# Top-k attention and a mixture of experts in one kernel: another order of all steps on every engine

## The chip, the cores and the metric

The kernel runs on one core of a Trainium2 chip. The metric is the device time of one launch in microseconds (us), from the start of the program to its end. The five engines of the core are named as in the profile: PE (TensorE, matrix products), DVE (VectorE), ACT (ScalarE), POOL (GpSimd) and SP (SyncE, which issues nearly all DMA transfers here). Each engine works off its own list of instructions in order; semaphores make it wait for the others.

## The reference

Attention of 2 batches, 8 heads, 576 rows and 64 columns per head, in which each row keeps only its 32 largest scores, is followed by a mixture of 4 experts on all 1152 rows:

```
scores = scale * np.matmul(q, k.transpose(0, 1, 3, 2))
kth = np.partition(scores, -top_k, axis=-1)[..., -top_k:-top_k + 1]      # top_k = 32
scores = np.where(scores >= kth, scores, -1000000000.0)
attn = np.exp(scores - np.max(scores, axis=-1, keepdims=True))
attn = attn / (np.sum(attn, axis=-1, keepdims=True) + 1e-09)
x = np.matmul(attn, v)                       # then heads side by side: x is 1152 x 512
p = domain_probs / (domain_probs.sum(-1, keepdims=True) + 1e-09)
for e in range(4):
    h = np.maximum(x @ w1[e], 0.0)           # w1[e]: 512 x 1024
    out += p[:, e:e + 1] * (h @ w2[e])       # w2[e]: 1024 x 512
```

All data is float32. The kernel splits each operand of a product into a high and a low half-precision part and adds three products (high by high, high by low, low by high).

## The kernel before

The 1152 rows are cut into ten row tiles (of 128 rows, and of 64 at the end of each batch). A tile of 128 rows has 8 units, one for each head; a 64-row tile has 4 units. There are 72 units, numbered 0 to 71 in the order of the tiles. A unit passes through these steps, each of them a small function that issues to one or two engines:

- `emit_qk` (PE, L643): scores of the unit into a PSUM bank. There are two such banks, so the scores of unit u need the bank that unit u-2 has left.
- `topk_op` (DVE, L656, L658 and L660): four rounds that find the 8 largest values (MAX8) with three that strike them out in between (MATCH_REPLACE).
- `emit_nb` (L693 on ACT, or L696 on DVE or POOL, by the table NB): the bias; `emit_exp` (ACT, L700): the exponential.
- `emit_mask` (L707 on DVE, or L710 and L714 on ACT and L717 on POOL): keeps the exponentials of the top 32. The table MASKS says for each unit which.
- `emit_a` (L725 on ACT, L727 and L729 on POOL): high and low part of the weights A.
- `emit_at` (SP, L735): transposes A with one DMA.
- `emit_av` (PE, L765): A times V into a PSUM bank for four heads. There is one such bank, which is free for the next four heads when `emit_x_half` (DVE, L785, L787, L789) has read it.

When a tile has all heads, its rows go through the experts: `m1` (PE, L882 to L884), the high part of h (ACT, L893), the low part (DVE L903, or ACT L900 and POOL L907, by the table H_LO), `m2` (PE, L929), and the evacuation with the expert's weight (by the table EVAC). The expert weights are loaded once: 16 loads of 1 MB (SP, L342). Each weight matrix has a power-of-two scale from its sum of squares, a chain over engines: Gram product of 32 matmuls (PE, L498), diagonal (DVE, L504), sum (PE, L507), then three small steps (DVE, L280, L282, L285). Then come the splits into high and low part (ACT L533, POOL L536). The queries of each tile are loaded and split likewise (L357, L373 to L402).

The order is written out by hand. Each step function is a generator; a step is entered in a heap with a place for each of its instructions, and all instructions are issued in the order of these places. The places are the numbers of the table ISSUE, one tuple per step and one number per instruction:

```
while events:
    place, i, n, f, args = heapq.heappop(events)
    ...
    heapq.heappush(events, (ISSUE[i][n] if ISSUE else place + (wait or 0), i, n, f, ()))
```

All five engines keep this order.

Of the kernel before, what the change touches and what calls it, by code (L numbers as in the profile page):

```python
# [43 lines left out]
H_LO = ('pddd', 'dppppppp', 'ppppdppp', 'dpppppdp', 'dpdpppdp', 'ppppdppd', 'pppppppp', 'pppppppp', 'pppdpppp', 'pppp')  # L44

MASKS = 'ddddddddddddddddrrdrrrrrrrrdrrrrrrrrrrrdrdrrrrdrrrrdrrdrrrrrrdrrrrrrrrrr'
NB = 'aaaadddddddaddadddddaadaadaapdddpppapppdpaaapapaaappppppapppppappaaaaaaa'
# [6 lines left out]
EVAC = ('ddpp', 'ddpp', 'dddp', 'ddpp', 'dppp', 'dpdd', 'dddd', 'dddd', 'dddd', 'dddd')  # L54
KV1 = dict(k='aaaaadaa', v='aaaaaaaa')
# [1197 lines left out]
```

## Time and profile before

| | |
|---|---|
| median of 3 runs | 539.23 us (539.05 to 540.62) |
| profiled execution | 540.16 us, of it 538.4 us span |
| busy share of the span | PE 94%, DVE 81%, ACT 68%, POOL 67% |
| chain of waits by engine | PE 78%, DVE 14%, DMA 2%, ACT 2%, SP 2% |
| mean granted TensorE clock | 0.977 of full speed |

The span runs from the first to the last instruction that the profiler recorded; the execution's own time is a little longer. A share of busy time is an average over stages that have different limits, so the profile is read by stretches of the span, and then by the lists of single instructions. In those lists the bracket at the end of a row is the idle time of the engine just before the instruction, and what ended it.

### The profile page before, as it was taken

The numbers are of one execution on the slowest core, as the hardware profiler recorded it, in microseconds if no ns is written. First come the engines' busy times: TensorE is split into PE (matmuls) and PEld (weight loads), VectorE is DVE, ScalarE is ACT, GpSimd is POOL, SyncE is SP. The second block draws the span as 40 slices with busy tenths as digits, with TensorE's granted clock in tenths as the row PEclk, the third lists the DMA queues.
The fourth block names the chain that finished last, engine by engine and source line by source line (L and its number), as shares of the span: only waits on it lengthen the run. The fifth ranks groups of instructions, "written<-read, shape, count | busy, mean of one in ns | idle before, by whom it ended". The sixth has DMA issues, their size and how long they took to land.

```text
span 538.4 us, 16332 instructions
## 1 busy us (share of the span) xinstructions
PE 505.1 (94%) x6738; PEld 384.6 (71%) x6738; DVE 433.7 (81%) x969; ACT 365.0 (68%) x602; POOL 361.4 (67%) x397
## 2 busy tenths in 40 slices
PE   7887758699999999999999999999999999999996
PEld 5666644586778677777777678677777778667766
DVE  3999997999999999999999989999999686610101
ACT  2999997998777777897768666764656635442121
POOL 0499997999877677978967866574665754253211
PEclk9997798799999999999999999999999999999999
DMA  8999998552474277574553642452423322214001
GB/s 218 311 255 331 265 280 170 104 90 47 99 144 75 65 111 128 94 139 93 122 113 88 110 70 66 83 89 45 76 52 62 71 45 47 43 24 65 12 2 32
DMA packets 142779, 58.37 MB, mean 108 GB/s; under 512 B 130096, under 2 KB 134448, under 8 KB 142704
## 3 DMA queue, kind: packets, MB, share of 16 engines
q1 hardware_dynamic: 139280, 54.50, 49.9%
q10 hardware_dynamic: 3424, 2.82, 1.7%
q8 instruction: 53, 0.87, 0.7%
q14 instruction: 22, 0.18, 0.1%
HBM read 25.45 MB, written 2.36 MB: 52 GB/s over the span
## 4 chain that ended last, share of the span: by engine, by line
PE 78%; DVE 14%; DMA 2%; ACT 2%; SPq 2%; issue 1%; POOL 0%; DVEq 0%
PE m L929 34%; PE m L882 11%; PE m L883 11%; PE m L884 11%; DVE m L656 6%; PE av L765 5%; PE ps L643 5%; DVE w L660 3%; DVE w L658 2%; DVE w L707 2%; DMA at<-a 2%; DMA pn<-in_moe_domain_probs_dram 1%; ACT w L533 1%; ACT w L527 1%; PE m L940 1%
## 5 line engine op out<-in xcount | busy, mean ns | idle before, releaser
L884 PE MATMUL m<-xt,w 128*128 128x128 f16 (+1 forms) x1280 | 199.8, 215 | 0.1
L929 PE MATMUL m<-w,h 128*128 128x512 f16 (+1 forms) x912 | 191.4, 383 | 0.0
L882 PE MATMUL m<-xt,w 128*128 128x128 f16 (+1 forms) x1120 | 178.9, 215 | 0.0
L883 PE MATMUL m<-xt,w 128*128 128x128 f16 (+1 forms) x1120 | 178.8, 215 | 0.0
L656 DVE MAX8 m<-w 128x8 f32<-128x576 f32 x216 | 161.6, 754 | 3.2
L929 PEld LDWEIGHTS <-h 128*128 128x128 f16 (+1 forms) x912 | 81.6, 101 | 88.4 <-issue 2.2
L884 PEld LDWEIGHTS <-w 128*128 128x128 f16 x1280 | 124.0, 99 | 0.2 <-POOL w L536 0.2
L882 PEld LDWEIGHTS <-w 128*128 128x128 f16 x1120 | 108.8, 99 | 2.6 <-issue 1.0
L907 POOL TENSOR_TENSOR h<-hf,h 128x512 f16<-128x512 f32 x59 | 68.4, 1160 | 62.6 <-ACT hf L900 62.2
L883 PEld LDWEIGHTS <-w 128*128 128x128 f16 x1120 | 108.5, 99 | 1.6
L660 DVE MATCH_REPLACE8 w<-m,w 128x576 f32<-128x576 f32 x144 | 106.9, 742 | 0.0
L727 POOL TENSOR_TENSOR a<-w,a 128x512 f16<-128x512 f32 x68 | 78.9, 1161 | 32.9 <-ACT a L725 17.9
L700 ACT ACTIVATE w<-ps,nb,es 128x576 f32<-128x576 f32 x68 | 56.3, 829 | 52.3 <-DVE m L656 46.1
L717 POOL TENSOR_TENSOR w<-w,d 128x576 f32<-128x576 f32 x48 | 61.4, 1282 | 27.6 <-ACT d L714 27.5
L893 ACT ACTIVATE h<-m 128x512 f16<-128x512 f32 x72 | 42.4, 593 | 53.5 <-PE m L884 35.9
L656 DVE MAX8 m<-ps 128x8 f32<-128x576 f32 x72 | 54.3, 755 | 15.2 <-PE ps L599 8.2
L725 ACT ACTIVATE a<-w 128x576 f16<-128x576 f32 x68 | 45.9, 679 | 13.2 <-POOL w L717 12.0
L658 DVE MATCH_REPLACE8 w<-m,ps 128x576 f32<-128x576 f32 x72 | 53.8, 747 | 0.0
L643 PE MATMUL ps<-kt,qa 128*128 128x288 f16 x128 | 34.9, 292 | 10.9 <-DVE w L707 10.0
L765 PEld LDWEIGHTS <-at 128*128 128x128 f16 (+1 forms) x1008 | 36.9, 101 | 9.1 <-DMA at<-a 3.5
L765 PE MATMUL av<-vt,at 128*128 128x65 f16 (+1 forms) x1008 | 39.4, 196 | 3.2 <-DMA at<-a 3.2
L900 ACT ACTIVATE hf<-m 128x512 f32<-128x512 f32 x59 | 34.9, 591 | 7.5 <-POOL h L907 6.0
(166 smaller groups left out, 759.1 us busy)
## 6 DMA issues: line engine op xcount, KB each, us to landing
w<-in_moe_w_dram SPq DMA_DIRECT2D x16, 1024.0 KB, 8.1
qraw<-in_q_dram SPq DMA_DIRECT2D x8, 256.0 KB, 3.4
qb<-qa SPq DMA_DIRECT2D x16, 128.0 KB, 2.6
out_dram<-o ACTq DMA_DIRECT2D x8, 256.0 KB, 2.2
at<-a SPq DMA_TRANSPOSE x68, 3.3
vraw<-in_v_dram SPq DMA_DIRECT2D x2, 512.0 KB, 7.4
nraw<-in_v_dram SPq DMA_DIRECT2D x4, 256.0 KB, 2.9
kraw<-in_k_dram SPq DMA_DIRECT2D x4, 256.0 KB, 2.9
```

What stands on the lines that cost most here:

```text
L643: PE.matmul(ps[:, 0:288], lhsT=src[:, x, :], rhs=kt[x].rearrange("p c n -> p (c n)")[:, ks], start=(j == 0), stop=(j == 1))
L656: DVE.max(m, s_t[u] if r == 0 else w_t[u])
L658: DVE.match_replace(rows2(w_t[u]), m, s_t[u], NEG)
L660: DVE.match_replace(w_t[u], m, w_t[u], NEG)
L717: POOL.tensor_tensor(w, w, g, op=OP.mult)
L727: POOL.tensor_tensor(a[:, 640:1152], w[:, 0:512], a[:, 0:512], op=OP.subtract)
L765: PE.matmul(o, lhsT=att[:, blk, ps], rhs=r, start=(i == 0), stop=(i == len(seq) - 1))
L882: PE.matmul(o, lhsT=HI[e, 0, c][:, fc], rhs=xs(0, c), start=(c == 0), stop=False)
L883: PE.matmul(o, lhsT=HI[e, 0, c][:, fc], rhs=xs(1, c), start=False, stop=False)
L884: PE.matmul(o, lhsT=LO[e, 0, c][:, fc], rhs=xs(0, c), start=False, stop=(c == 3))
L907: POOL.tensor_tensor(h[:, 1], hf, h[:, 0], op=OP.subtract)
L929: PE.matmul(y[z * 64:z * 64 + M, :], lhsT=h_t[es, qd][:, p // 2, h0:h0 + M], rhs=w, start=(fc == 0 and p == 0), stop=(fc == 7 and p == 2))
```

## The change

Only tables change: ISSUE as a whole, and five smaller tables that say which engine does a step. By count, DVE has three more low parts of h (16 for 13), three evacuations fewer (14 for 17) and one mask fewer (23 for 24); the number of biases on DVE falls from 20 to 19. Every computed value stays the same. The diff of the small tables, and the first rows of ISSUE:

```
-H_LO = ('pddd', 'dppppppp', 'ppppdppp', 'dpppppdp', 'dpdpppdp', 'ppppdppd', 'pppppppp', 'pppppppp', 'pppdpppp', 'pppp')
+H_LO = ('pddd', 'dppppppd', 'dpppddpp', 'dpdppdpp', 'ppdpppdp', 'ppppdppd', 'pppppdpp', 'pppppppp', 'pppppppp', 'pppp')
-MASKS = 'ddddddddddddddddrrdrrrrrrrrdrrrrrrrrrrrdrdrrrrdrrrrdrrdrrrrrrdrrrrrrrrrr'
+MASKS = 'ddddddddddddddddrrdrrrrrrrrrrrrrrdrrrrdrrddrrrrdrrrrrrrrrrrdrrrrrrrrrrrr'
-EVAC = ('ddpp', 'ddpp', 'dddp', 'ddpp', 'dppp', 'dpdd', 'dddd', 'dddd', 'dddd', 'dddd')
+EVAC = ('ddpp', 'dppp', 'dppp', 'ddpd', 'dppp', 'dpdp', 'dddd', 'dddd', 'dddd', 'dddd')
-KV1 = dict(k='aaaaadaa', v='aaaaaaaa')
+KV1 = dict(k='aaaaaaaa', v='aaaaaaaa')
 ISSUE = [
-    (0,), (9,), (10,), (48,), (54,), (1, 2), (3, 4), (20, 23), (36, 47), (25, 28), (12,), (13, 14), (19, 22, 32, 39),
...
+    (1,), (7,), (9,), (42,), (59,), (0, 2), (3, 4), (20, 24), (35, 46), (30, 34), (12,), (13, 15), (18, 22, 28, 60),
...
```

NB, the table of the engine of each bias, changes in the same manner. What the numbers do is seen in the order of the instructions.

On PE, in the ramp, before the change. A row is a source line, an instruction, what it writes and what it reads. `m1_1173` and `m1_1255` take the Gram products of two weight matrices, `w30_907` and `w21_128`; `av_1210` is the A·V bank of units 4 to 7, and `at_1039`, `at_1245` and `at_1251` are the transposed weights of units 5, 6 and 4; `ps0_1295` takes the scores of unit 11; `m2_1324` is an expert product of the first tile (24 matmuls).

```order
L498 MATMUL m1_1173<-w30_907 128x128
...
L765 MATMUL av_1210<-vt_139,at_1039 128x65
...
L498 MATMUL m1_1255<-w21_128 128x128
...
L643 MATMUL ps0_1295<-kt7_138,qa_398 128x288
...
L765 MATMUL av_1210<-vt_139,at_1245 128x65
...
L507 MATMUL m1_1255<-gd_1293,ones_112 128x1
...
L929 MATMUL m2_1324<-w10_125,h_1165 64x512
...
L765 MATMUL av_1210<-vt_139,at_1251 128x65
...
L507 MATMUL m1_1173<-gd_1362,ones_112 128x1
```

The same place after the change; `at_1154`, `at_1165` and `at_1199` are those of units 5, 6 and 4, `ps0_1194` and `ps0_1304` the scores of units 10 and 11, and `m2_1349` is the expert product.

```order
L765 MATMUL av_1173<-vt_139,at_1154 128x65
...
L643 MATMUL ps0_1194<-kt6_137,qa_445 128x288
...
L498 MATMUL m1_1211<-w21_128 128x128
...
L498 MATMUL m1_1247<-w30_1026 128x128
...
L507 MATMUL m1_1211<-gd_1281,ones_112 128x1
...
L765 MATMUL av_1173<-vt_139,at_1165 128x65
...
L643 MATMUL ps0_1304<-kt7_138,qa_445 128x288
...
L765 MATMUL av_1173<-vt_139,at_1199 128x65
...
L507 MATMUL m1_1247<-gd_1312,ones_112 128x1
...
L929 MATMUL m2_1349<-w10_125,h_1171 64x512
```

The expert product stood ahead of the second L507 and now stands behind it; the scores of unit 11 stood ahead of the A·V product of unit 6 and now stand behind it; the scores of unit 10, which before stood ahead of all these rows, have both Gram products behind them.

On SP, the DMA issues of the same stretch before the change, with no row left out. `w21`, `w30` and `w31` are loads of expert weights, `at` the transposed weights of units 5, 6 and 4, `qa` a transpose of queries. `kt6_137` and a load of queries stand some rows ahead of it.

```order
L342 DMA w21_128<-in_moe_w2_dram 128x4x512
L342 DMA w30_907<-in_moe_w1_dram 128x2x1024
L735 DMA_TRANSPOSE at_1039<-a_816 128x9x128
L342 DMA w30_907<-in_moe_w1_dram 128x2x1024
L342 DMA w21_128<-in_moe_w2_dram 128x4x512
L342 DMA w31_908<-in_moe_w2_dram 128x4x512
L735 DMA_TRANSPOSE at_1245<-a_1043 128x9x128
L394 DMA_TRANSPOSE qa_1248<-qhl_881 128x8x128
L735 DMA_TRANSPOSE at_1251<-a_814 128x9x128
```

And after the change, the same stretch:

```order
L342 DMA w21_128<-in_moe_w2_dram 128x4x512
L735 DMA_TRANSPOSE at_1154<-a_826 128x9x128
L342 DMA w30_1026<-in_moe_w1_dram 128x2x1024 x2
L735 DMA_TRANSPOSE at_1165<-a_1011 128x9x128
L357 DMA qraw_1168<-in_q_dram 128x8x64
L394 DMA_TRANSPOSE qa_1188<-qhl_847 128x8x128
L735 DMA_TRANSPOSE at_1199<-a_822 128x9x128
L342 DMA w31_1027<-in_moe_w2_dram 128x4x512
```

The first load of `w31` stood ahead of the transpose of unit 6 and now stands behind that of unit 4; the load of queries also moves behind the transpose of unit 6.

On PE, far behind the ramp, before the change. `ps0_6204` takes the scores of unit 53, `av_6257` is the A·V bank of units 48 to 51, `at_6140` is of unit 48 and `at_6434` of unit 49:

```order
L643 MATMUL ps0_6204<-kt1_132,qa_5510 128x288
...
L929 MATMUL m2_6212<-w10_125,h_5870 128x512
...
L765 MATMUL av_6257<-vt_139,at_6140 128x65
...
L643 MATMUL ps0_6332<-kt2_133,qa_5510 128x288
...
L765 MATMUL av_6257<-vt_139,at_6434 128x65
```

And after the change; `av_6170` is the A·V bank of units 48 to 51, `at_6089` is of unit 49 and `at_6202` of unit 48, `ps0_6190` takes the scores of unit 53:

```order
L765 MATMUL av_6170<-vt_139,at_6089 128x65
...
L643 MATMUL ps0_6190<-kt1_132,qa_5505 128x288
...
L882 MATMUL m1_6210<-xt_5765,w11_126 128x128
...
L643 MATMUL ps0_6291<-kt2_133,qa_5505 128x288
...
L765 MATMUL av_6170<-vt_139,at_6202 128x65
```

Unit 49 was the last of its four to go through A·V and is now the first, and stands just ahead of the scores of unit 53.

## Rows read from the trace of the kernel before

**Rows 1.** Stretches: from:to, length, busy us (instructions) PE, PEld, DVE, ACT, POOL; PEclk, DMA, GB/s.

```profile
60.00:80.00 20.00, 13.63 (x288) 12.50 (x286) 19.76 (x49) 19.78 (x23) 19.67 (x14) 0.92 1.15 281
80.00:90.00 10.00, 10.00 (x111) 5.95 (x108) 6.45 (x22) 6.95 (x9) 9.82 (x10) 0.83 0.99 205
90.00:120.00 30.00, 21.30 (x418) 19.12 (x416) 29.79 (x71) 28.79 (x34) 27.03 (x20) 0.89 0.56 102
120.00:200.00 80.00, 80.00 (x988) 58.70 (x986) 78.27 (x177) 61.21 (x109) 62.76 (x67) 1.00 0.49 88
...
300.00:400.00 100.00, 100.00 (x1257) 75.43 (x1256) 93.54 (x191) 62.73 (x109) 65.45 (x81) 1.00 0.41 74
```

**Rows 2.** Pieces of the chain of waits: start, length (both us), what.

```profile
71.40 8.36 DMA at<-a
...
117.84 0.73 DVE w L707
...
118.61 0.65 PE ps L643 x4
```

**Rows 3.** DVE's list: start, length, line, operation, out<-in, shapes; idle before.

```profile
78.26 0.75 DVE L656 MAX8 m<-ps 128x8 f32<-128x576 f32 x1
...
85.72 0.16 DVE L280 TENSOR_SCALAR wpt<-m 128x1 int32<-128x1 int32 x1 [3.55 <-PE m L507]
```

**Rows 4.** PE's list from 79 to 90 us.

```profile
79.81 0.76 PE L765 MATMUL av<-vt,at 128*128 128x65 f16 x14 [3.21 <-DMA at<-a]
...
80.87 4.07 PE L929 MATMUL m<-w,h 128*64 128x512 f16 x24
...
85.33 0.36 PE L507 MATMUL m<-gd,ones 128*128 128x1 f32 x2
...
86.56 2.78 PE L929 MATMUL m<-w,h 128*64 128x512 f16 x24
```

**Rows 5.** Two weight loads: SP's list, then the transfers' KB and us to landing.

```profile
63.69 0.72 SPq L342 DMA_DIRECT2D w<-in_moe_w_dram  x1
64.46 1.62 SPq L342 DMA_DIRECT2D w<-in_moe_w_dram  x1
...
w<-in_moe_w_dram SPq DMA_DIRECT2D x1, 1024.0 KB, 10.2
...
w<-in_moe_w_dram SPq DMA_DIRECT2D x1, 1024.0 KB, 12.0
```

**Rows 6.** POOL: a weight split from its list; its longest wait, 80 to 128 us.

```profile
62.17 2.14 POOL L536 TENSOR_TENSOR w<-w 128x1024 f16<-128x1024 f32 x1 [0.23 <-ACT w L533]
...
POOL a L727 <- ACT a L725: 2.7, 1, 2.7
```

**Rows 7.** ACT's waits, 82 to 100 us: us in total, times, longest.

```profile
ACT w L527 <- PE ps L643: 1.5, 1, 1.5
ACT w L700 <- DVE wpt L280: 1.2, 1, 1.2
ACT w L700 <- DVE m L656: 1.1, 1, 1.1
ACT a L725 <- DMA at<-a: 0.4, 1, 0.4
```

**Rows 8.** The squares of v of the second batch: ns min/median/max, first and last start.

```profile
L461 ACT ACTIVATE nraw<-nraw x4: 720/728/757, 132.5 to 200.4; 128x640 bf16<-128x640 f32 x4
```

**Rows 9.** Lists of POOL, PE, DVE and SP, 329 to 346 us; the transpose's landing.

```profile
329.32 1.16 POOL L907 TENSOR_TENSOR h<-hf,h 128x512 f16<-128x512 f32 x1 [0.88 <-ACT hf L900]
...
335.34 0.29 PE L643 MATMUL ps<-kt,qa 128*128 128x288 f16 x1
...
339.51 0.41 DVE L789 TENSOR_TENSOR x<-av,r 128x256 f32<-128x256 f32 x1
...
345.25 2.32 SPq L735 DMA_TRANSPOSE at<-a  x1
...
at<-a SPq DMA_TRANSPOSE x1, 3.8
```

More of the change, by code (lines that the diff above doesn't have):

```diff
@@ L43 @@
 MANUAL = ('PE', 'DVE', 'Activation', 'Pool', 'SP')
-H_LO = ('pddd', 'dppppppp', 'ppppdppp', 'dpppppdp', 'dpdpppdp', 'ppppdppd', 'pppppppp', 'pppppppp', 'pppdpppp', 'pppp')
-MASKS = 'ddddddddddddddddrrdrrrrrrrrdrrrrrrrrrrrdrdrrrrdrrrrdrrdrrrrrrdrrrrrrrrrr'
-NB = 'aaaadddddddaddadddddaadaadaapdddpppapppdpaaapapaaappppppapppppappaaaaaaa'
+H_LO = ('pddd', 'dppppppd', 'dpppddpp', 'dpdppdpp', 'ppdpppdp', 'ppppdppd', 'pppppdpp', 'pppppppp', 'pppppppp', 'pppp')
+MASKS = 'ddddddddddddddddrrdrrrrrrrrrrrrrrdrrrrdrrddrrrrdrrrrrrrrrrrdrrrrrrrrrrrr'
+NB = 'aaaaddddddaddaadaddddpdpdadppadpapppaaapppppadaappdaaaaaaapapaaaaaapapaa'
 X_LO = 'pppppppppp'
```

316 rows, old and new, of the table ISSUE are left out of this document.

## Prediction

> **What bounds the kernel now.** I first read the busy time of each engine by stretches [rows 1]. From 60 to 80 us DVE is busy for 19.76 of 20 us while PE has 13.63; from 90 to 120 us DVE has 29.79 of 30 and PE 21.30. From 120 us on PE is full (80.00 of 80). So there are two stages: a ramp, in which DVE's top-k sets the pace, and a long stage in which TensorE never waits. The second begins where the chain of waits passes from DVE to PE [rows 2]: the mask of unit 15 starts on DVE at 117.84, the scores of unit 17 (L643, into the bank that this mask had read) start on PE at 118.61, and from there the chain is PE's until the end. The change leaves PE's work in the second stage as it is. So the time falls by as much as that mask ends earlier, provided that PE is fed as well as before.
>
> In the ramp there is one hole: from 80 to 90 us DVE is busy for 6.45 of 10 us [rows 1]. DVE's own list of instructions shows why [rows 3]: its L280, the first step of a weight scale, waits 3.55 us for PE's L507. PE's list tells what is ahead of that L507 [rows 4]: the A·V product of unit 6 (L765), which waited 3.21 us for its transposed weights and started at 79.81, then 24 matmuls L929 of the expert layer, 4.07 us of them, then A·V of unit 4, and only then, at 85.33, the L507. The same 24 matmuls take 2.78 us a little later; the granted clock from 80 to 90 us is 0.83 of full speed [rows 1], so part of the 4.07 is the clock after the idle time. The transpose of unit 6 was issued on SP at 71.40 and landed 8.36 us later [rows 2]. Ahead of it SP had issued 1 MB weight loads, the last two at 63.69 and 64.46, which landed 10.2 and 12.0 us later, at 73.9 and 76.5 [rows 5]. So the hole has two causes, a transpose behind weight loads and an L507 behind 24 matmuls.
>
> **What the change does there.** On PE the 24 matmuls move behind the second L507, and both Gram products L498 move behind the scores of unit 10. On POOL the two subtractions that finish unit 6 move ahead of three weight splits (2.1 us each, [rows 6]) and a q split. On SP the transpose of unit 6 then follows two loads of w30 and nothing else that is new: one 1 MB load and a q load fewer are ahead of it.
>
> When does that transpose land? Nothing in the trace shows it with this queue, so I bound it. At the earliest it takes 3.8 us as one on a freer queue does [rows 9]. It can be issued when POOL has finished unit 6: three splits and one more such step earlier than 71.4, some 7.5 us, so at about 63.9, and lands at 67.7. At the latest it lands as before, at 79.76. The loads landed 2.6 us apart; with one fewer ahead the last of them lands at 73.9, and the transpose at most 3.3 us later, as before (79.76 − 76.5): 77.2. DVE wants the scores of unit 11, now behind that A·V product, at about 77.6: before, this MAX8 started at 78.26 [rows 3], and one MATCH_REPLACE of 0.74 us that was ahead of it is now behind. With 0.76 us for A·V [rows 4] and 0.65 for the scores [rows 2] the transpose must be there by 76.2. At 77.2 it costs 1.0 us, at 76.2 or earlier nothing. The L507 is wanted four top-k instructions of 0.7 us after 77.6, at about 80.4. With the 24 matmuls no longer ahead it needs only A·V of unit 4, whose transpose follows some 2 us behind (2.32 us is what SP takes to issue one, [rows 9]): at the latest 77.2 + 2.0 + 0.76 + 0.36 = 80.3, so it fits too.
>
> The Trainium skill, in "DMA: Bandwidth & Descriptors", section "Queues, rings and completion order", says that completion is not in order of issue for one issuing engine. By that the transpose need not wait for the loads ahead of it at all; here the landings of 73.9, 76.5 and 79.76 came in the order of issue [rows 2, 5]. By the rule the transpose would land near 67.7 and the first rival below would lose its chance; the sum below would stay, since it is capped elsewhere.
>
> **The sum.** On DVE the hole of 3.55 us goes, and ahead of the mask of unit 15 stand two reciprocals and two biases fewer and one L280 more, about 0.1 us each (an L280 is 0.16 us, [rows 3], and overlaps its neighbour): 3.55 + 0.3 = 3.9, less at most 1.0 for the late transpose, gives 2.9 to 3.9. But DVE is not alone. ACT works almost without a gap in the ramp; between 82 and 100 us it waited 1.5, 1.2, 1.1 and 0.4 us [rows 7], 4.2 in all, and can give back no more than these. The change puts one squaring of v (0.72 us and about 0.2 for its sum, [rows 8]) and small things of 0.2 ahead of the exponential of unit 15: 3.1 are left. POOL waited 2.7 us once, for ACT [rows 6], and has the same 73 instructions ahead of the last weight split, which PE needs early in the second stage: 2.7 and a little more. I take 2.8.
>
> Later, in the stage where PE is full, one step is tight. The A·V product of unit 49 moves eleven steps forward on PE, to just ahead of the scores of unit 53, which started at 335.34 [rows 9]. It is now the first to write the one A·V bank, and so must wait for DVE's L789 to have read the half before, which ended at 339.92 [rows 9]. The change moves that L789 ahead of three MAX8 and two MATCH_REPLACE, 5 × 0.75 = 3.75 us, so it ends at about 336.1, against 335.3 for PE. Both clocks are shifted alike by what the ramp gives. PE then loses 0 to 0.8 us here; I take 0.4. DVE's other edits (three lo parts more, three evacuations and one mask fewer) lie in the second stage, where DVE had 6 us of 100 free [rows 1], and cost nothing as long as no PE step waits for DVE there.
>
> The profiled execution took 540.16 us (span 538.4), 0.93 above the median of 539.23. 540.16 − 2.8 + 0.4 = 537.8 on its own basis; less 0.93 this is **536.8**. Its own range is 535.6 to 537.8. Measurements of this kernel tell about 0.3% (1.62 us) from no change.
>
> **Rivals.** First, the wait moves instead of going (chance 0.27). The scores of unit 11 now stand behind the A·V product of unit 6, which before was behind them. If the transpose lands as late as before, 79.76, DVE gets these scores at 81.0 instead of 77.6 and loses 3.4 of the 3.55 us at a new place: 539.0. For it speaks that the queue ahead is still full of weight loads (the DMA engines moved 281 GB/s from 60 to 80 us, [rows 1]); against it, that one load fewer is ahead. Gain 0 to 2 us, time 537.2 to 539.2.
>
> Second, slower (0.17): the moved A·V product of unit 49 holds PE. Besides the L789 it needs its own transpose, which before was issued at 345.25 and took 3.8 us [rows 9]. Its POOL part now stands where POOL started at 329.32 after a 0.88 us wait for ACT; with 1.5 us of its own, such a wait and 3.8 us of transfer it lands at about 335.5, with no margin. Each us after 335.3 costs PE one. At 338.1 the gain is eaten, at about 339.7 the kernel is slower by 0.3%, and half-way to the old landing of 349.0, at 342.2, the time would be 543.3 (536.4, the forecast without its 0.4, and 6.9). Against it: ACT and POOL are busy for only 63 and 65% there [rows 1], so a late unit can catch up.
>
> Third, more than the caps (0.10): ACT's and POOL's waits shrink because their inputs come earlier too, and all of 3.9 to 4.2 us comes back: 535.0.
>
> **How the numbers follow.** The forecast has 0.46. Faster by over 0.3% (below 537.6): 0.43 of the forecast, 0.10 of the third, 0.06 of the first: 0.59. Within 0.3%: 0.20 of the first, 0.03 and 0.02 at the edges: 0.25. Slower: 0.16. The range runs from 534.8, just below the third rival's price, to 540.6, near the point at which slower begins; some 0.15 lies beyond that, 0.02 below.
>
> **What would show it.** In the profile after: no idle time over 1 us on DVE between 60 and 118 us, the L507 of the w30 Gram product before the 24 matmuls and at about 80; the transpose of unit 6 issued near 64 and landed by 77; the mask of unit 15 starting near 115; PE without a gap from there on, and none over 1 us before the scores of unit 53. If DVE waits for L643 at about 78, the first rival is right; if PE waits over 3 us for a transpose or for L789 near 333, the second. What would make it wrong altogether is a wait in the second stage behind one of the many steps that move there by a place or two.

## The result, and the profile after

The changed kernel is slower: a median of 544.7 us (4 runs, 543.68 to 545.99) beside 539.14 us for the kernel before in the same set (4 runs, 538.35 to 540.62), a ratio of 1.0101 with a 95% interval of 1.0066 to 1.0136. The forecast was 536.8 with a range up to 540.6. Timed once more in ten runs it gave 1.0070 (1.0044 to 1.0097). The profiled execution took 545.63 us, its span is 543.8.

One mark in the program splits the span well: the first matmul of the scores of unit 17, at which the chain of waits passes from DVE to PE. It stood at 118.61 us before and stands at 116.89 now, 1.7 earlier, so the ramp did become shorter in this execution. But from there to the end it took 419.8 us before and takes 426.9 now: 7.1 lost in the stage that the forecast held to be unchanged. −1.7 + 7.1 is the difference of the two spans, 5.4.

First the stretches of the changed kernel, with the columns of [rows 1].

```profile
60.00:80.00 20.00, 15.46 (x304) 13.93 (x304) 20.00 (x53) 20.00 (x26) 20.00 (x15) 0.89 1.18 269
80.00:90.00 10.00, 9.13 (x84) 4.71 (x85) 10.00 (x30) 10.00 (x12) 10.00 (x10) 0.83 1.24 305
90.00:120.00 30.00, 22.57 (x452) 21.07 (x451) 29.68 (x70) 29.58 (x37) 30.00 (x22) 0.94 0.62 103
120.00:200.00 80.00, 80.00 (x986) 58.50 (x984) 78.46 (x177) 61.72 (x106) 62.92 (x71) 1.00 0.46 84
...
220.00:230.00 10.00, 8.13 (x124) 7.08 (x122) 8.52 (x18) 6.40 (x14) 7.19 (x10) 1.00 0.28 61
230.00:240.00 10.00, 8.45 (x76) 7.26 (x76) 7.11 (x19) 7.68 (x17) 6.08 (x9) 0.66 0.55 119
```

DVE is now busy for 10.00 of the 10 us from 80 to 90 (6.45 in [rows 1]): the hole is gone. What is new stands in the last two rows: PE, full until 220, has 1.87 us free in one stretch and 1.55 in the next, and the clock granted in the second is 0.66 of full speed, a mean between the two levels. Next come PE's waits between 118 and 530 us (engine and line, what it waited for, us in total, times, longest); the kernel before has none there.

```profile
PE ps L643 <- ACT d L710: 1.9, 1, 1.9
PE m L440 <- ACT kt L433: 0.8, 1, 0.8
PE m L882 <- ACT hf L900: 0.7, 1, 0.7
```

Three waits, each for ACT, 3.4 us in all. The clock takes the rest: 10 us at 0.66 are worth 3.4 us. The sum, 6.8, is nearly the whole loss of 7.1. The chain of waits (columns of [rows 2]) tells where ACT's lateness comes from.

```profile
116.12 0.74 DVE w L707
116.89 0.65 PE ps L643 x4
...
224.75 5.16 DMA at<-a
229.93 0.04 ACT d L710
...
230.57 0.55 ACT kt L433 x2
...
232.20 0.58 PE m L440 x2
```

The transpose issued at 224.75 is that of unit 31 and lands 5.16 us later. ACT's mask of unit 34 cannot start before it has landed, and PE's scores of unit 36 wait for that mask. One step further back, the instruction lists of the changed kernel (SP, then ACT, then POOL; columns of [rows 3]):

```profile
214.26 0.38 SPq L325 DMA_DIRECT2D kraw<-in_k_dram  x1
214.70 1.66 SPq L328 DMA_DIRECT2D kraw<-in_k_dram  x1
216.53 1.31 SPq L735 DMA_TRANSPOSE at<-a  x1
223.55 0.39 SPq L325 DMA_DIRECT2D kraw<-in_k_dram  x1
...
224.75 1.28 SPq L735 DMA_TRANSPOSE at<-a  x1
...
219.83 0.68 ACT L725 ACTIVATE a<-w 128x576 f16<-128x576 f32 x1 [3.26 <-DMA at<-a]
...
229.93 0.74 ACT L710 ACTIVATE d<-ps,m 128x576 f32<-128x576 f32 x1 [2.63 <-DMA at<-a]
...
220.59 1.17 POOL L727 TENSOR_TENSOR a<-w,a 128x512 f16<-128x512 f32 x1 [2.79 <-ACT a L725]
...
222.36 1.17 POOL L388 TENSOR_TENSOR qhl<-qraw,qhl 128x512 f16<-128x512 f32 x1
```

The keys of the second batch are loaded two heads at a time (`kraw`, L325 and L328); these loads are called k pairs here. SP now issues the load of k pair 1 ahead of the transpose of unit 30, which goes out at 216.53 and lands at 219.75. ACT's copy of unit 31 (L725) waits 3.26 us for that landing. POOL's lo part of the same unit waits 2.79 behind it, then comes the q split L388, and only then does SP get the raw buffer for the load of k pair 2 (223.55), which now stands ahead of the transpose of unit 31 (224.75). In the kernel before SP has the two in the other order:

```profile
214.22 1.30 SPq L735 DMA_TRANSPOSE at<-a  x1
215.62 0.52 SPq L325 DMA_DIRECT2D kraw<-in_k_dram  x1
...
220.42 1.30 SPq L735 DMA_TRANSPOSE at<-a  x1
...
222.47 0.39 SPq L325 DMA_DIRECT2D kraw<-in_k_dram  x1
```

Counted from the scores of unit 17, the transpose of unit 30 went out at 95.6 us (214.22 − 118.61) and now goes at 99.6 (216.53 − 116.89).

Why does a copy of unit 31 wait for the transpose of unit 30? Copies and masks share a pool of three buffers. The two programs deal them out so (in the order in which they are taken; X, Y and Z are the buffers' addresses):

```
before:   mask 31 X   copy 30 Z   mask 32 Y   copy 31 X   copy 32 Z   mask 33 Y   mask 34 X
changed:  copy 30 Y   mask 31 X   mask 32 Z   copy 31 Y   copy 33 X   mask 34 Y   copy 32 Z
```

In the changed kernel the copy of unit 30, the copy of unit 31 and the mask of unit 34 stand one behind the other in buffer Y, so the second needs the landing of the first one's transpose, and the third that of the second's. Before, the copy of unit 31 took over from a mask, and ACT waited for no landing in this stretch.

### The profile page after: what moved, and what is told of

Its sections match the earlier page's. It is cut to its first block, busy times and chain, and to the rows that moved or that the text cites. A ratio compares the mean times of both kernels' runs of the same rounds, so it can differ in the third digit from the quotient of the medians.

```text
span 543.8 us, 16334 instructions
## 1 busy us (share of the span) xinstructions
PE 512.0 (94%) x6738; PEld 389.3 (72%) x6738; DVE 433.5 (80%) x966; ACT 367.2 (68%) x610; POOL 361.6 (66%) x395
## 4 chain that ended last, share of the span: by engine, by line
PE 78%; DVE 16%; ACT 2%; DMA 2%; issue 1%; SPq 0%; ACTq 0%
PE m L929 33%; PE m L882 11%; PE m L883 11%; PE m L884 11%; DVE m L656 7%; PE av L765 5%; PE ps L643 5%; DVE w L660 3%; DVE w L658 2%; DVE w L707 2%; DMA at<-a 1%; PE ps L599 1%; ACT w L527 1%; ACT w L533 1%; DMA qraw<-in_q_dram 1%
## 5 line engine op out<-in xcount | busy, mean ns | idle before, releaser
L884 PE MATMUL m<-xt,w 128*128 128x128 f16 (+1 forms) x1280 | 202.2, 216 | 1.6 <-POOL w L536 1.6
L882 PE MATMUL m<-xt,w 128*128 128x128 f16 (+1 forms) x1120 | 181.6, 216 | 0.7 <-ACT hf L900 0.7
L883 PE MATMUL m<-xt,w 128*128 128x128 f16 (+1 forms) x1120 | 181.5, 216 | 0.0
L907 POOL TENSOR_TENSOR h<-hf,h 128x512 f16<-128x512 f32 x56 | 65.0, 1160 | 56.9 <-ACT hf L900 49.6
L717 POOL TENSOR_TENSOR w<-w,d 128x576 f32<-128x576 f32 x49 | 62.8, 1282 | 38.9 <-ACT d L714 38.6
L725 ACT ACTIVATE a<-w 128x576 f16<-128x576 f32 x68 | 45.8, 679 | 16.3 <-POOL w L717 9.1
L976 DVE SCALAR_TENSOR_TENSOR o<-m,pniw,o 128x512 f32<-128x512 f32 (+1 forms) x13 | 9.7, 746 | 56.2 <-PE m L929 46.7
```

Source lines behind the costliest of these rows:

```text
L717: POOL.tensor_tensor(w, w, g, op=OP.mult)
L882: PE.matmul(o, lhsT=HI[e, 0, c][:, fc], rhs=xs(0, c), start=(c == 0), stop=False)
L883: PE.matmul(o, lhsT=HI[e, 0, c][:, fc], rhs=xs(1, c), start=False, stop=False)
L884: PE.matmul(o, lhsT=LO[e, 0, c][:, fc], rhs=xs(0, c), start=False, stop=(c == 3))
L907: POOL.tensor_tensor(h[:, 1], hf, h[:, 0], op=OP.subtract)
```

## The experiments

In the tables of numbers, 766 and 773 are the transposes of units 30 and 31, 765 the copy of unit 30, 771 and 779 the masks of units 31 and 32 (their second numbers are the mask's second half on ACT, the third the product on POOL), 1173 the 24 matmuls of the first tile. "Start" is the start of the scores of unit 17 in the profiled execution, "rest" the span less start. Lines are shifted by one to nine in kernels with added lines.

### The second stage

**The changed kernel with the two transposes ahead of the two loads**, twice (e1 and e10 are the same edit).

```
+ISSUE[766] = (1071.5,)        # was 1090; the load of k pair 1 is 1072
+ISSUE[773] = (1102.5,)        # was 1107; the load of k pair 2 is 1103
```

> The changed kernel with two of SP's issues back where they stood before: the transpose of unit 30 ahead of the load of k pair 1, that of unit 31 ahead of the load of k pair 2. Theory A (SP's queue: the transpose of unit 31 stands behind a load that waits 5.6 us for POOL, lands 6.3 us later than before, and ACT and then PE wait for it): PE's waits of 0.7, 1.9 and 0.8 us near 225 to 232 go, the granted clock from 230 to 240 stays at 1.00, and the 6.4 us that the changed kernel loses from 225 to 255 come back: 544.7 - 6.4 = 538.3. Theory B (ACT's own order: unit 31's copy now takes the buffer of unit 30, so it waits for that transpose wherever it stands on SP): PE still waits 1 us or more for ACT there and the time stays above 541.

> The changed kernel with the transposes of units 30 and 31 ahead of the two loads, once more, for its time. Stretch behind the scores of unit 17 at 419.9 us; the ramp is shorter than in the kernel before by 1 to 2 us: median 1 to 2 us under the kernel before, ratio 0.996 to 0.999. If the ramp gives nothing on average: ratio 1.000.

Measured: ratios to the kernel before of 0.9991 (0.9960 to 1.0022, 10 runs) and 1.0010 (0.9984 to 1.0035, 12 runs); rest 419.9 us both times. PE has no wait between 118 and 530 us. Stretches of e1:

```profile
220.00:230.00 10.00, 10.00 (x167) 9.15 (x165) 9.52 (x23) 8.24 (x21) 8.00 (x12) 1.00 0.36 87
230.00:240.00 10.00, 10.00 (x122) 7.07 (x119) 9.29 (x22) 9.02 (x17) 7.79 (x12) 1.00 0.97 151
```

And ACT's one wait for a landing there, from its waits:

```profile
ACT a L727 <- DMA at<-a: 1.1, 1, 1.1
```

The copy of unit 31 still waits, but 1.1 us is hidden; PE is full. So the loss sits in these two steps of SP's order. And since rest is now that of the kernel before, these 22 runs also time the changed ramp by itself: it is worth nothing that can be measured.

**One transpose moved back at a time.**

```
e5: +ISSUE[766] = (1071.5,)
e6: +ISSUE[773] = (1102.5,)
```

> The changed kernel with only the transpose of unit 30 back ahead of the load of k pair 1; that of unit 31 stays behind the load of k pair 2. The length to look at is that from the scores of unit 17 to the end: 419.8 us in the kernel before, 426.9 in the changed kernel, 419.9 with both transposes back. If the chain starts at unit 30 (ACT's copy of unit 31 waits for its landing, POOL's part of the copy and the q split wait for ACT, the load of k pair 2 for POOL, the transpose of unit 31 for the load), landing some 2 us earlier moves all of it by 2 us and PE's waits shrink below 0.5 us: 420 to 422. If only unit 31's own place counts: 425 to 427.

> The changed kernel with only the transpose of unit 31 back ahead of the load of k pair 2; that of unit 30 stays behind the load of k pair 1. If the link from the load to the transpose of unit 31 is needed for the loss, that transpose is issued at about 222.5 (when POOL has its part of unit 31) instead of 224.8, lands before 227, and ACT's mask of unit 34 does not wait: 420 to 421 from the scores of unit 17 to the end. If the late unit 30 alone is enough: PE still waits and 424 or more.

Measured: rest 420.1 us with unit 30's alone and 421.2 with unit 31's alone (one execution each, 540.65 and 540.85 us). Unit 30's gives all of it back: the chain begins there. With unit 31's alone ACT's copy still waits 3.2 us, but only 0.7 reaches PE, so the loss needs the second link too, the load of k pair 2 ahead of the transpose of unit 31.

**The same order of SP in the kernel before.**

```
+ISSUE[766] = (1059.5,)        # was 1055; behind the load of k pair 1
+ISSUE[773] = (1091.5,)        # was 1070; behind the load of k pair 2
```

> The kernel before with the same two places of SP turned round: the transposes of units 30 and 31 behind the loads of k pairs 1 and 2. Theory A: SP's order alone is enough, PE waits 2 us or more between 220 and 235 and the time is 542 to 545. Theory B: the kernel before takes other buffers there and does not need these landings early: no PE wait, 539 to 540.

Measured: 1.0004 (0.9968 to 1.0039, 10 runs), rest 420.3. PE's only wait in the stage is this:

```profile
PE av L767 <- DMA at<-a: 0.3, 1, 0.3
```

SP's order costs half a microsecond where the copy of unit 31 stands in another buffer. So it needs a partner in the changed order. The test is not quite a full one: here the transpose of unit 30 goes out 97.6 us after the scores of unit 17 (217.10 − 119.47), half as late as in the changed kernel (95.6 before, 99.6 changed).

**The copy of unit 30 behind the mask of unit 31**, which was meant to break a dependence between the two.

```
+ISSUE[765] = (1032.2, 1033.0, 1034.0)        # was (1023, 1031, 1034); mask 31 is 1032
```

> The changed kernel with SP's order as it is, but ACT's copy of unit 30 behind its mask step of unit 31, as in the kernel before. Then the copy of unit 31 takes the buffer of that mask and not the one that the transpose of unit 30 still reads. Theory B (the buffer order on ACT is the second condition): ACT's wait of 3.3 us for the transpose of unit 30 at 216.6 goes or moves, the load of k pair 2 starts some 3 us earlier, and 420 to 422 from the scores of unit 17 to the end. If SP's order alone decides: 426 to 427.

Measured: rest 423.3 us (one execution, 541.58 us), ACT waits 2.8 and 2.2 us for landings as before, PE 2.7 in all. A miss, and the buffer table says why: the pool deals the copies of units 30 and 31 and the mask of unit 34 into one buffer again, X instead of Y.

**The mask of unit 32 behind the copy of unit 31**, in the changed kernel.

```
+ISSUE[779] = (1064.5, 1064.7, 1101)        # was (1046, 1054, 1101); copy 31 is 1064
```

> The changed kernel with ACT's mask of unit 32 put behind its copy of unit 31; SP's order stays as changed. In the built program the copy of unit 31 then stands in the buffer of the copy of unit 28, whose transpose has landed long before, and no longer in that of unit 30. Theory (one buffer for the copies of units 30 and 31 and the mask of unit 34, and SP's late transposes): ACT's copy of unit 31 no longer waits for a landing near 216 to 220 us, the load of k pair 2 and the transpose of unit 31 are issued some 3 us earlier, PE has at most 0.8 us of waits between 118 and 300 us, and the time from the scores of unit 17 to the end is 419.8 to 420.8 us instead of 423.6 to 426.9; the time goes to that of the kernel before within 0.4%. Rival (SP's order is enough beside the changed order of ACT, whatever the buffers): the waits stay and that time is 423 or more.

Measured: 1.0046 (1.0017 to 1.0074, 12 runs), rest 424.1. ACT waits for no landing any more between 205 and 240 us, as the theory had it; but the rest did not fall, since PE has a new wait:

```profile
PE ps L644 <- ACT d L711: 2.4, 1, 2.4
```

That is the scores of unit 34 waiting for the mask that I moved, and the clock granted from 220 to 230 us was 0.83. The edit took one wait away and made another, so its time decides nothing.

**The shared buffer put into the kernel before**, with SP's loads first (e14) and with SP's own order (e15).

```
e14: +ISSUE[766] = (1059.5,)
     +ISSUE[773] = (1091.5,)
     +ISSUE[771] = (1026.5, 1030, 1058)        # was (1017, 1030, 1049)
e15: +ISSUE[771] = (1026.5, 1030, 1058)
```

> The kernel before with the loads of k pairs 1 and 2 ahead of the transposes of units 30 and 31 on SP, and with the mask of unit 31 begun behind the copy of unit 30 and ended behind that of unit 31, by which the copies of units 30 and 31 and the mask of unit 34 stand in one buffer. Theory (buffer chain and SP's order together make the loss): ACT's copy of unit 31 waits 2 to 4 us for the transpose of unit 30, PE has 2 to 4 us of waits between 210 and 240 us, and the time from the scores of unit 17 to the end is 422 to 424 us (420.3 with SP's order alone); with a fall of the clock behind it up to 427. Rival (something else in the changed order of ACT): it stays at 419.8 to 420.8.

> The kernel before with the same two places of the mask of unit 31 and SP's own order, transposes ahead of loads; the copies of units 30 and 31 stand in one buffer here too. Theory: ACT's copy waits for the transpose of unit 30 at most 1.5 us, as with the transposes first in the changed kernel, no wait reaches PE, and the time from the scores of unit 17 to the end is 419.8 to 420.3 us. Rival (the one buffer costs by itself): 422 or more.

Measured: e14 1.0139 (1.0091 to 1.0187, 4 runs), rest 427.7; e15 541.86 us in one execution, rest 424.7. Both are longer than I expected; e15 came out as the rival said (the one buffer costs by itself) and not as the theory. POOL's list of e15 shows a cost of the edit itself:

```profile
216.98 1.28 POOL L718 TENSOR_TENSOR w<-w,d 128x576 f32<-128x576 f32 x1 [3.78 <-ACT a L726]
```

At 1058 POOL's product of unit 31 stands behind ACT's copy of the same unit (the lo part taken after it makes up for that in the values) and must wait until the copy has read; the copy waits 2.4 us for the transpose of unit 30 (3.5 in e14), and so POOL stands idle for 3.78 us. The shared buffer does make ACT's copy wait in this order too, but what it costs by itself can't be read from these two.

**The clean test: another buffer for the copy of unit 31 by one swap.** In the changed kernel, with SP's order as changed, the second half of the mask of unit 31 goes one place forward on ACT, ahead of the first half of the mask of unit 32, and its product one place forward on POOL, ahead of a bias of 0.3 us. That is enough for the pool to give the copy of unit 31 buffer X, the mask's, instead of Y.

```
+ISSUE[771] = (1032, 1045.5, 1045.7)        # was (1032, 1052, 1057); mask 32 is 1046
```

> The changed kernel, SP's order as changed, with two neighbours swapped: on ACT the second half of the mask of unit 31 ahead of the first half of the mask of unit 32, on POOL the product of the mask of unit 31 ahead of one bias of 0.3 us. In the built program the copy of unit 31 then takes the buffer of the mask of unit 31 instead of that of the copy of unit 30; the mask of unit 34 still takes the buffer of the copy of unit 31. Theory (the shared buffer turns SP's late transpose into the loss): ACT's copy of unit 31 does not wait for a landing, PE's waits between 124 and 300 us fall from 2.7 to 3.4 us to at most 1, the time from the scores of unit 17 to the end is 419.8 to 421.0 us instead of 423.2 to 426.9, and the ratio to the kernel before is 0.998 to 1.003. Rival (the late transposes and the late load of k pair 2 are enough by themselves): 423 or more, ratio 1.006 or more.

Measured: **0.9986 (0.9963 to 1.0009, 12 runs, median 538.27 us beside 538.78)**, rest 420.0 us. PE has no wait between 118 and 530 us. Its stretches:

```profile
220.00:230.00 10.00, 10.00 (x171) 9.37 (x170) 9.51 (x25) 7.97 (x19) 7.35 (x13) 1.00 0.37 89
230.00:240.00 10.00, 10.00 (x121) 7.07 (x119) 9.27 (x21) 8.84 (x16) 7.76 (x11) 1.00 0.93 155
```

And its lists of SP and then ACT around the place:

```profile
213.70 0.38 SPq L326 DMA_DIRECT2D kraw<-in_k_dram  x1
...
215.63 1.31 SPq L736 DMA_TRANSPOSE at<-a  x1
220.22 0.38 SPq L326 DMA_DIRECT2D kraw<-in_k_dram  x1
...
215.96 0.68 ACT L726 ACTIVATE a<-w 128x576 f16<-128x576 f32 x1
```

The transpose of unit 30 goes out as late as in the changed kernel (215.63 − 116.33 = 99.3 us after the scores of unit 17), but the copy of unit 31 runs at 215.96, while that transpose is still under way, and the load of k pair 2 goes out 2.8 us earlier than in the changed kernel, counted from the same mark (220.22 − 116.33 = 103.9 against 223.55 − 116.89 = 106.7). The swap by itself brings nothing forward: in the changed kernel ACT had done all that stood ahead of the copy at 216.57 (219.83 less the wait of 3.26), 99.7 us after the mark, and here the copy starts 99.6 after it. The whole loss is gone with one swap. It is the buffer that turns SP's late transpose into a wait; either half may be taken away.

**The changed kernel twice more, and with the waits filled.** e9 and e16 are the changed kernel as it is. e4 adds matmuls on PE whose results nothing uses, where it waited: 18 ahead of the scores of unit 36 and 8 ahead of a sum of the key scales.

```
+        def fill(n):
+            for _ in range(n):
+                PE.matmul(av_t[(0, 384, 128), 0][:, 260:512], lhsT=HI[0, 1, 0][:, 0:128],
+                          rhs=HI[0, 1, 0][:, 0:252], start=True, stop=True)
...
+            if u == 36:
+                fill(18)
...
+                if hs[0] == 4:
+                    fill(8)
```

> The changed kernel once more, unaltered. If the loss behind the scores of unit 17 is a property of its order: PE waits again for ACT near 225 to 232, and that stretch is 423 us (the waits alone) to 427 us (waits and a fall of the clock) against 419.8 before; median 543 to 545. If it was an accident of one execution: 420 and 538 to 539.

> The changed kernel as it is, a third profiled execution. Theory: the waits of PE for ACT's mask of unit 34 and the key pieces behind it are there again, 2.5 to 3.5 us in sum; the time from the scores of unit 17 to the end is 423.6 us if the clock stays at full speed between 220 and 240 us and 425 to 427 if it falls, which I put at one in three. Rival (the waits were rare): 420.

> The changed kernel with 18 matmuls that compute nothing put ahead of the scores of unit 36 and 8 ahead of the sum of k pair 2 (L440), on PE, into an unused part of the A.V bank: they lie in PE's waits near 229 and 231. If the fall of the granted clock to 0.66 from 230 to 240 comes from PE's idle time there, the clock stays near 1.00 and some 3 of the 6.4 us come back: 541.5 to 542. If the clock falls for another reason, or the waits alone cost it all: 544 to 545.

Measured: e9 1.0070 (1.0044 to 1.0097, 10 runs), rest 423.6; e16 541.54 us in one execution, rest 423.2; e4 1.0070 (1.0034 to 1.0105, 10 runs), rest 423.4. The waits of PE in e9 and e16 are nearly those of the first execution (3.1 and 2.7 us beside 3.4), but the clock did not fall behind them in e9 and e16, as these two stretches of e9 show:

```profile
220.00:230.00 10.00, 9.53 (x102) 6.79 (x101) 9.06 (x21) 6.15 (x13) 7.08 (x10) 1.00 0.38 82
230.00:240.00 10.00, 7.41 (x116) 6.14 (x113) 7.16 (x19) 6.92 (x17) 6.46 (x10) 1.00 0.42 91
```

So the waits cost 3.4 to 3.8 us each time (423.2 or 423.6 less 419.8), and the fall of the clock added 3.3 in one of three executions. e4 had full clock too, but so had two executions without filling: whether filling prevents the fall stays open.

### The ramp

**The kernel before once more**, as it is.

> The kernel before once more, for a second profile of its ramp. If the hole of 3.55 us on DVE belongs to its order: DVE waits again 2.5 us or more in sum between 78 and 92 us. The stretch behind the scores of unit 17 is 419.8 us again; what differs between executions lies in the ramp.

Measured: 537.88 us in one execution, start 116.24, rest 419.9. The hole on which the forecast rests isn't there. Stretches of this execution:

```profile
75.00:80.00 5.00, 4.02 (x62) 3.22 (x60) 4.97 (x12) 4.76 (x6) 5.00 (x4) 1.00 1.29 177
80.00:85.00 5.00, 4.63 (x60) 2.73 (x58) 5.00 (x16) 5.00 (x9) 5.00 (x5) 1.00 1.00 204
```

PE's list, then DVE's L280:

```profile
78.53 0.62 PE L765 MATMUL av<-vt,at 128*128 128x65 f16 x14 [0.66 <-DMA at<-a]
...
79.31 2.78 PE L929 MATMUL m<-w,h 128*64 128x512 f16 x24
82.47 0.36 PE L507 MATMUL m<-gd,ones 128*128 128x1 f32 x2
...
83.37 0.14 DVE L280 TENSOR_SCALAR wpt<-m 128x1 int32<-128x1 int32 x1
```

The same order of instructions, yet DVE is full from 80 to 85 us and L280 waits for nothing. The transpose of unit 6 landed 1.3 us earlier and the 24 matmuls took 2.78 us instead of 4.07 [rows 4]. e14 and e15 have this ramp too, with 0 and 0.2 us of waits on DVE between 60 and 122 us; e2 has 2.8.

**The ramp's edits one at a time**, in the kernel before: the 24 matmuls behind the second L507 (e3), or behind both and further on (e8); and in the changed kernel with the transposes first, the same matmuls a little later, behind the A·V product of unit 7 (e12).

```
e3:  +ISSUE[1173] = (381.5,)        # was 364
e8:  +ISSUE[1173] = (396.5,)        # was 364
e12: +ISSUE[766] = (1071.5,)
     +ISSUE[773] = (1102.5,)
     +ISSUE[1173] = (369.5,)        # was 368
```

> The kernel before with one step moved: the 24 expert matmuls (L929) of the first tile that stood ahead of the second L507 in the ramp stand behind it. If the hole of 3.55 us on DVE is due to these matmuls: the L507 comes at about 82.2 instead of 85.3, the hole shrinks to 0.5 us or less and the mask of unit 15 ends some 3 us earlier; time 539.1 - 2.8 = 536.3 by the caps of ACT and POOL in the prediction. Rival: what the ramp gives is taken back by a later wait or by the clock: 538 to 540.

> The kernel before with the 24 expert matmuls of the ramp moved further than in the earlier run: behind the second L507, the A.V product of unit 7 and the scores of unit 13, so that neither the L507 nor that product (for which DVE waited 3.0 us when they stood ahead of it) waits for them. If these matmuls made the hole of 3.55 us: no DVE wait over 0.6 us near 82 to 88, the scores of unit 17 start at 115.5 to 117 instead of 118.6, the rest stays at 419.8 us, and the median falls by 2 to 3 us against the kernel before. If something else takes the gain (the clock, ACT or POOL): scores of unit 17 at 118 or later, median within 1 us.

> The changed kernel with the two transposes first, and with the 24 expert matmuls of the ramp also behind the A.V product of unit 7, for which DVE waited 1.6 to 2.0 us near 86 in three of six executions of the changed ramp. If that wait is the rest of the old hole: none there, scores of unit 17 at 116 to 116.7, median 2 to 3 us under the kernel before (ratio 0.994 to 0.997). If PE's matmuls only push the wait to the next step (as it was when they were moved in the kernel before): a DVE wait of 1 to 2 us near 90 to 96, and no gain over the other run of this call.

Measured: e3 1.0045 (1.0011 to 1.0080), e8 1.0013 (0.9986 to 1.0040), ten runs each; e12 1.0068 (1.0038 to 1.0097, 9 runs) with its start at 125.01. In each of them DVE waits in the ramp for another step: 3.0 us for an A·V product in e3, 2.3 for scores in e8, and in e12:

```profile
DVE m L659 <- PE ps L646: 4.9, 2, 4.7
DVE r L788 <- PE av L768: 2.1, 1, 2.1
DVE wpt L283 <- PE m L510: 1.2, 1, 1.2
```

No place of the 24 matmuls that I tried shortened the ramp: e3 and e12 made the kernel slower, and e8, where they stand later than in e3, can't be told from the kernel before.

All profiled executions but those of e3, e8 and e12, in us: the wait of ACT's copy of unit 31 for a landing, and PE's waits between 124 and 300 us in sum:

```
kernel                         start    rest    ACT copy 31   PE waits
before                        118.61   419.8        0             0
before again (e11)            116.24   419.9        0             0
loads first in before (e2)    119.47   420.3        0           0.3
e15                           115.45   424.7      2.4           2.8
e14                           114.20   427.7      3.5           4.6
changed                       116.89   426.9      3.3           3.4
changed again (e9)            120.18   423.6      3.0           3.1
changed, third (e16)          116.47   423.2      2.7           2.7
e7                            116.50   423.3      2.8           2.7
e4 (filled)                   119.12   423.4      3.0           0.5
e6                            117.88   421.2      3.2           0.7
e5                            118.76   420.1      1.2             0
transposes first (e1)         116.68   419.9      1.1             0
transposes first (e10)        118.07   419.9      1.4             0
e13                           119.48   424.1        0           2.4
one swap (e17)                116.33   420.0        0             0
```

The five executions with the old ramp (the first five lines) start at 114.2 to 119.5, 116.8 in the mean; the eleven with the changed ramp at 116.3 to 120.2, 117.9 in the mean.

## Why the prediction was wrong, point by point

**The hole and its causes.** In the one execution that was profiled the reading held: the transpose of unit 6 was issued at 65.95 (forecast near 64) and landed at 75.28, by the 76.2 that was wanted; L507 came at 80.96 ("at about 80") ahead of the 24 matmuls; DVE had no wait over 1 us. PE and DVE of the changed kernel there, beside [rows 3, 4]:

```profile
80.51 0.62 PE L765 MATMUL av<-vt,at 128*128 128x65 f16 x14 [0.93 <-DMA at<-a]
80.96 0.36 PE L507 MATMUL m<-gd,ones 128*128 128x1 f32 x2
81.25 4.47 PE L929 MATMUL m<-w,h 128*64 128x512 f16 x24
...
82.47 0.14 DVE L280 TENSOR_SCALAR wpt<-m 128x1 int32<-128x1 int32 x1
```

It landed in order of issue again: two weight loads ahead of it at 71.58 and 74.19, the transpose at 75.28. Completion out of order, which the Trainium skill's page "DMA: Bandwidth & Descriptors", section "Queues, rings and completion order", allows for, was not needed to explain it and did not show.

**The first step that failed: "On DVE the hole of 3.55 us goes", and 2.8 of it as the gain.** The 3.55 us were read from one execution and taken for a property of the order. In four other executions of the same ramp DVE's waits there were 0, 0, 0.2 and 2.8 us. The two of these five executions with such waits are those with a lower granted clock just there (0.66 from 80 to 85 us in the first, 0.62 from 75 to 80 in e2; the other three show 1.00 from 75 to 85). The changed order has waits at other steps in five of its eleven executions: 1.7 us for an A·V product and 1.1 for L507 in e9 and in e5, 1.6 to 2.0 for an A·V product in e4, e6 and e13. So the first rival's outcome, that the wait moves, came in about half of them, but not at the place that it named: for the scores of unit 11 DVE waited 0.4 us at most.

The other part of that term, 0.3 us less of DVE's own work ahead of the mask, had the wrong sign. Three instructions fewer do stand there, but from the start of the span to the start of the scores of unit 17 DVE was busy for 104.9 to 105.2 us in the five executions with the old ramp and for 105.6 to 106.1 in the eleven with the changed one, 0.8 more in the mean; it was idle for 11.8 and 12.0 us in the mean. About all of the 0.8 is one instruction, L1075, a scale of the first batch's keys. First its row in the kernel before, then it and POOL's L388 in the changed kernel:

```profile
15.80 0.22 DVE L1075 TENSOR_SCALAR invk<-ones,k0pr 128x8 f32<-128x8 f32 x1
...
22.87 0.83 DVE L1075 TENSOR_SCALAR invk<-ones,k0pr 128x8 f32<-128x8 f32 x1
22.52 1.16 POOL L388 TENSOR_TENSOR qhl<-qraw,qhl 128x512 f16<-128x512 f32 x1 [20.93 <-ACT qhl L383]
```

In the new order it runs beside POOL's L388 and ends with it, at 23.70 beside 23.68. It takes 0.22 to 0.23 us in all five executions with the old ramp and 0.8 to 1.2 in all eleven with the changed one. Why it lasts until POOL's step ends was not tested.

So the profiled pair shows 1.7 us of gain, 2.3 less of idle time on DVE and 0.6 more of work, and it was the luck of that pair: the timed kernels with the changed ramp and a whole second stage show none (0.9991, 1.0010 and 0.9986, each interval holding 1). The term was −2.8 us; it measured 0, within 0.3% (1.6 us) or so. (A slip in the first rival's price changes nothing: 79.76 + 0.76 + 0.65 is 81.2 and not 81.0.)

**The second step that failed: "Later, in the stage where PE is full, one step is tight."** I looked for a tight step among PE's and DVE's moves and priced that of unit 49. The tight place was on ACT and SP: two transposes behind two loads, and a buffer that passes from copy to copy. The term that was missing is 3.4 to 3.8 us from the waits, and 3.3 more from the clock when it falls. The sentence that DVE's edits cost nothing as long as no PE step waits for DVE held; PE waited for ACT. That a wait in the second stage "behind one of the many steps that move there" would make the forecast wrong was written down, but none of these steps was followed.

**Unit 49.** The 0.4 us put on its place did not come: PE has no wait there in the changed kernel. The second rival had the right kind of cause, a transpose that comes too late for a PE that is full, but at the wrong unit and by another path: it went over ACT's buffer, not over the A·V product itself. That its time for the case half-way (543.3) is near the measured 544.7 is luck.

**The caps** of ACT and POOL were not tested, since no gain came that they could cap.

## What to carry to other kernels

A stall that one execution shows is not yet a property of the order: profile the kernel before a second time before pricing its hole. When a new order moves a transfer on a queue, follow not only who reads what it brings but who takes over the buffer that it reads from: a pool deals its buffers by the order of the steps, so a swap of two neighbours can make or break a wait that no line of the code shows; the addresses of the tiles in the built program show it. And where an engine has no slack, go through the moves on every engine that feeds it, with the most attention to those that issue DMAs.

## What the runs showed of the hardware that I had not expected

Executions of one kernel differ by several us (535.9 to 542.3 for the kernel before in 29 of the 31 runs of one set), and in the profiled ones the difference lies in the ramp: start ranges over 5 us in the five with the old ramp, while rest is 419.7 to 420.1 in all nine executions without a wait of PE in the second stage.

The same waits of PE in the second stage were followed by a granted clock of 0.66 over 10 us in one execution of the changed kernel and by full clock in two others. e13, e14 and e15, whose waits of 2.4 to 4.6 us lie around 216 to 228 us, had 0.79 to 0.84 from 220 to 230.

In the ramp the granted clock from 80 to 85 us was 0.50 to 0.71 in all eleven executions with the changed order, and the 24 matmuls took 3.8 to 5.3 us; in the old order they took 2.78 us in four of five, at full clock. e3 and e8, which move only these matmuls in the kernel before, show 0.66 and 0.50 there as well. So the move of the 24 matmuls goes with the lower clock in these runs. But e12, in which they start only at 89.86, shows 0.59 from 80 to 85 us too, so they need not stand there for it. Why the clock falls was not settled.
